# Merging page lists and gathering rows earlier in the last pages of a spectral mixture-of-experts kernel

## The chip, the cores and the metric

The kernel runs on one core of a Trainium2 chip. The metric is device time in microseconds, the median of several executions. Five engines work side by side, each through its own instructions in order: PE (TensorE, matrix multiplication), DVE (VectorE), ACT (ScalarE), POOL (GpSimd, which here issues the indirect transfers) and SP (SyncE, which issues most other transfers). PEld in the profile is the weight load of a matmul, which overlaps other matmuls.

## The reference

```python
def reference(**kwargs):
    # x: 8 x 3072 x 256
    X = np.fft.fft(x, axis=1); X = np.fft.fft(X, axis=2); x = X.real.reshape(24576, 256)
    # mixture of experts, top 1 of 8
    xn = x / (norm(x) + 1e-6); en = expert_emb / (norm(expert_emb) + 1e-6)
    logits = xn @ en.T / tau
    idx = argmax(logits); gate = softmax(logits)[idx]
    for e in range(8):
        out[idx == e] = gate * (relu(x[idx == e] @ w1[e]) @ w2[e])   # 256 -> 1024 -> 256
    # dense layer
    h = out @ w_in                                                   # 256 -> 2048
    return maximum(0.01 * h, h) @ w_out                              # 2048 -> 256
```

## The kernel before, in words

**Batches and routing.** For each of eight batches the transform is computed as matrix products, the result `xo` is stored to a table `xd` of 24576 rows in device memory, and each row is routed: its expert, its slot among that expert's rows and its gate are found, and three tables receive by scatter, at the row's slot, the row's number and gate. Each of the three holds a third of the entries; everywhere else stands a very large number.

**Pages.** A page is 256 slots of one expert. `load_page` (SP) reads the page's stretch of the three tables into a tile `t3`, `t` in the profile. `fetch_page` then does two things: DVE takes the minimum of the three (lines 872 and 873) and casts the row numbers to integers (line 878, tile `tab`), and POOL gathers the rows with an indirect transfer from `xd` into one of two buffers `xr`, 128 rows at a time (line 895). `transpose` turns the rows by PE (line 924) and splits them by ACT and DVE into a high and a low part (lines 926, 927, tile `xt`), since each product is made of three passes. 89 pages (`NFULL`) are full pages. What is left of the eight experts is computed in 21 half pages of 128 slots (numbers 89 to 109), with one gather each; their results pass through `yd` to seven last dense pages.

**Steps.** `steps` is a list of triples (kind, page, part). Kind 1 is the expert's layers of a full page, 4 steps; kind 3 those of a half page, 2 steps; kind 2 the dense layer, 8 steps. The loop goes over steps. At step `i` it first runs the hooks registered for `i`, then the first product of the step (kind 1: line 939, kind 2: line 1012, kind 3: line 971) with its work on ACT and DVE, then the second product (lines 957, 1043, 984) of the step three earlier (`LAG`). So PE does two groups of products in each step, and what ACT and DVE make of the first is needed three steps later. In kind 3 PE transposes the intermediate result as well (line 1028). From page 79 on, one full page and two half pages take turns: in the list of steps ten full pages (79 to 88) are at steps 944, 960, 976 and so on every 16, with a half page 7 and 12 steps behind each.

**Hooks.** For the page that is n-th in this order and begins at step `i`, `load_page` is registered at step `k`, 13 steps ahead of `i` (`AHEAD`) but not before the page before last has begun, or 7 ahead (`NEAR`) for the first ten. `fetch_page` follows by the line that the change touches. `transpose` stands at `i - 2`. The page's weights come as four pieces of 512 KB through two buffers `raw` (lines 906, 908, on SP, in the order of the hooks with the list loads) and are split by ACT and DVE (lines 917, 918) into `w1` and `w2`: for the full pages in turn with half pages the first two pieces at `i - 2` and `i - 1`.

An engine takes its instructions in the order in which the loop records them, so a hook's step sets the place on every engine that it uses.

Of the kernel before, what the change touches and what calls it, by code (L numbers as in the profile page):

```python
# [37 lines left out]
GAP = 1  # L38
# [20 lines left out]
class K:  # L59
# [770 lines left out]
    def main(self):  # L830
# [17 lines left out]
        for j in range(2, NFULL):  # L848
# [6 lines left out]
            if first <= j < NFULL - PRE + 1 and tail:  # L855
                left_pages = NFULL - PRE + 1 - j
                n = -(-len(tail) // left_pages)
# [199 lines left out]
        def at(i, fn, *args):  # L1057
            hooks.setdefault(max(0, i), []).append((fn, args))
# [3 lines left out]
        for n, (i, u) in enumerate(firsts):  # L1062
            ip_ = firsts[n - 1][0] if n else -8
            if n >= 2:
                k = max(firsts[n - 2][0] + 1, i - (NEAR if n < 10 else AHEAD))
                at(k, load_page, u)
                at(min(k + (GAP if n < 10 else 5), i - 3), fetch_page, u)
            if n:

                na = 4 if firsts[n - 1][1] < NFULL else 2  # L1070
                s0, s1 = ip_ + na, min(ip_ + na + 1, i)
                s2, s3 = ip_ + na // 2 + LAG + 1, min(ip_ + na + LAG, i + LAG)
                at(max(ip_ + 1, ls[0]), wload, u, 0)
                at(max(ip_ + 2, ls[1]), wload, u, 1)
                at(s0, wsplit, u, 0)
                at(s0, wload, u, 2)
                at(s1, wsplit, u, 1)
                at(s1, wload, u, 3)
                at(s2, wsplit, u, 2)
                at(s3, wsplit, u, 3)  # L1080
                ls = (s2, s3)
                at(max(i - 2, ip_ + na), transpose, u)
        last = firsts[-1][0]
        for t in range(NTF):
            i = [k for k, s in enumerate(steps) if s == (2, NU + t, 0)][0]
# [14 lines left out]
        with tc.tile_pool(name="ip", bufs=1) as self.ip:  # L1100
# [5 lines left out]
            for lab in g0:  # L1106
                n = count[lab] = count.get(lab, 0) + 1
                k, every = RAMP.get(lab, (0, 1))
# [61 lines left out]
        for i in range(len(steps) + LAG):  # L1170
# [8 lines left out]
            if i < len(steps):  # L1179
                m, u, s = steps[i]  # L1180
# [6 lines left out]
            while done < len(steps) and i - done >= (LAG if done > 4 * PRE else 2):  # L1187
                m, u, s = steps[done]
# [144 lines left out]
```

## Time and profile before

| | us |
|---|---|
| median of three runs | 3794.94 |
| lowest, highest | 3792.76, 3804.19 |
| profiled execution | 3783.82 |
| its span | 3782.1 |
| PE busy in the span | 3590.3 (95%) |
| DVE busy | 2338.3 (62%) |
| ACT busy | 1936.0 (51%) |
| POOL busy | 677.7 (18%) |

The mean granted clock of TensorE over the span is 0.971 of full speed. Busy time is summed over the whole span; what a stage waits for has to be read in that stage. In the rows, a bracket or the part behind the last bar tells how long an engine was idle before an instruction and what ended that. "SPq" is the issue of a transfer by SP.

### The profile page before, as it was taken

The numbers are of one execution on the slowest core, as the hardware profiler recorded it, in microseconds if no ns is written. First come the engines' busy times: TensorE is split into PE (matmuls) and PEld (weight loads), VectorE is DVE, ScalarE is ACT, GpSimd is POOL, SyncE is SP. The second block draws the span as 40 slices with busy tenths as digits, with TensorE's granted clock in tenths as the row PEclk, the third lists the DMA queues.
The fourth block names the chain that finished last, engine by engine and source line by source line (L and its number), as shares of the span: only waits on it lengthen the run. The fifth ranks groups of instructions, "written<-read, shape, count | busy, mean of one in ns | idle before, by whom it ended". The sixth has DMA issues, their size and how long they took to land. (4 is left out here: it accounts for less than half of the span.)

```text
span 3782.1 us, 74898 instructions
## 1 busy us (share of the span) xinstructions
PE 3590.3 (95%) x29441; PEld 3554.3 (94%) x29441; DVE 2338.3 (62%) x4595; ACT 1936.0 (51%) x3491; POOL 677.7 (18%) x620
## 2 busy tenths in 40 slices
PE   4488999999999999999999999999999999999998
PEld 3388999999999999999999999999999988988998
DVE  7575656567565666567565666657675556655544
ACT  3345446545555446455554456554645555555543
POOL 3113110411122101311023110311113111110000
PEclk8699999999999999999999999999999999999999
DMA  4332413232223223233233322232322244444300
GB/s 137 122 105 70 140 61 115 74 116 75 95 88 105 96 72 104 72 111 93 75 101 77 122 85 91 76 121 79 110 64 84 88 129 135 136 139 127 103 25 16
DMA packets 266165, 362.58 MB, mean 96 GB/s; under 512 B 75984, under 2 KB 216659, under 8 KB 265620
## 3 DMA queue, kind: packets, MB, share of 16 engines
q1 hardware_dynamic: 238896, 303.66, 25.6%
q0 software_dynamic: 25184, 52.35, 4.5%
q8 instruction: 230, 3.77, 0.4%
q10 hardware_dynamic: 1732, 1.79, 0.1%
q14 instruction: 123, 1.01, 0.1%
HBM read 304.64 MB, written 63.41 MB: 97 GB/s over the span
## 5 line engine op out<-in xcount | busy, mean ns | idle before, releaser
L1043 PE MATMUL o<-wo,hh 128*128 128x256 f32 x9216 | 1240.7, 284 | 10.1 <-DVE hh L1032 10.1
L1012 PE MATMUL h<-yt,wi 128*128 128x256 f32 x9216 | 1232.9, 283 | 13.5 <-ACT yt L961 13.4
L1043 PEld LDWEIGHTS o<-wo,hh 128*128 128x128 f32 x9216 | 1157.3, 190 | 13.8 <-DVE hh L1032 10.6
L1012 PEld LDWEIGHTS h<-yt,wi 128*128 128x128 f32 x9216 | 1152.5, 191 | 14.0 <-ACT yt L961 13.6
L1014 ACT ACTIVATE g<-h 128x512 f32<-128x512 f32 x768 | 457.8, 596 | 833.8 <-PE h L1012 827.8
L1015 DVE TENSOR_TENSOR g<-g,h 128x512 f32<-128x512 f32 x768 | 526.3, 685 | 509.7 <-ACT g L1014 508.7
L918 DVE TENSOR_TENSOR w<-raw,w 128x1024 fp32r<-128x1024 f32 x440 | 536.9, 1224 | 156.1 <-ACT w L917 153.3
L1050 POOL DMA_INDIRECT out<-ob,tab x192 | 216.9, 1130 | 2238.6 <-ACT ob L1049 1876.9
L942 DVE SCALAR_TENSOR_TENSOR hh<-h,hh 128x512 fp32r<-128x512 f32 x356 | 246.2, 692 | 559.7 <-ACT hh L941 558.3
L939 PE MATMUL h<-xt,w 128*128 128x256 f32 x4272 | 573.9, 284 | 16.4 <-ACT xt L926 14.0
L957 PE MATMUL y<-hh,w 128*128 128x256 f32 x4272 | 579.2, 285 | 8.5 <-ACT w L917 7.6
L939 PEld LDWEIGHTS h<-xt,w 128*128 128x128 f32 x4272 | 539.4, 192 | 18.0 <-ACT xt L926 14.9
L957 PEld LDWEIGHTS y<-hh,w 128*128 128x128 f32 x4272 | 541.5, 192 | 10.1 <-ACT w L917 8.0
L1032 DVE TENSOR_TENSOR hh<-g,hh 128x512 fp32r<-128x512 f32 x768 | 525.4, 684 | 1.1 <-ACT hh L1031 1.0
L917 ACT ACTIVATE w<-raw 128x1024 fp32r<-128x1024 f32 x440 | 461.8, 1054 | 85.5 <-DMA raw<-w 83.8
L1031 ACT ACTIVATE hh<-g 128x512 fp32r<-128x512 f32 x768 | 479.6, 625 | 25.4 <-DVE g L1015 25.3
L941 ACT ACTIVATE hh<-h 128x512 fp32r<-128x512 f32 x356 | 212.8, 598 | 529.0 <-PE h L939 528.9
L895 POOL DMA_INDIRECT xr<-xd,tab x199 | 235.9, 1185 | 685.1 <-issue 357.3
L597 POOL DMA_INDIRECT table<-tb,sli x192 | 217.8, 1135 | 170.3 <-DVE tb L591 56.6
L924 PE MATMUL a<-ident,xr 128*128 128x128 f32 x426 | 73.8, 290 | 81.9 <-DMA xr<-xd,tab 81.5
L924 PEld LDWEIGHTS a<-ident,xr 128*128 128x128 f32 x426 | 52.1, 146 | 87.1 <-DMA xr<-xd,tab 44.3
L1049 ACT ACTIVATE ob<-o,tf 128x256 f32<-128x256 f32 x192 | 80.6, 471 | 76.5 <-PE o L1043 76.4
(291 smaller groups left out, 1790.8 us busy)
## 6 DMA issues: line engine op xcount, KB each, us to landing
raw<-w SPq DMA_DIRECT2D x440, 512.0 KB
x<-xl SPq DMA_DIRECT2D x32, 768.0 KB
xd<-xo SPq DMA_DIRECT2D x96, 256.0 KB
table<-bigd SPq DMA_DIRECT2D x21, 384.0 KB
t<-table SPq DMA_DIRECT2D x267, 4.0 KB
xr<-xd,tab POOLq DMA_INDIRECT x199, 4.5
table<-tb,sli POOLq DMA_INDIRECT x192, 3.6
rawz<-w_out SPq DMA_DIRECT2D x6, 512.0 KB
```

The lines of the kernel that those rows point to most:

```text
L895: nc.gpsimd.indirect_dma_start(out=self.xr[seq[u] % NX][:, h], out_offset=None, in_=self.xd[0:rows, :], in_offset=bass.IndirectOffsetOnAxi ...
L917: nc.scalar.activation(hi, r, AF.Copy)
L918: V.tensor_tensor(lo, r, hi.bitcast(F32), op=ALU.subtract)
L939: nc.tensor.matmul(p[:, f], self.w1[:, wa, dc, fc * 128:(fc + 1) * 128], xt[:, xa, dc], start=(k == 0), stop=(k == 5))
L942: V.scalar_tensor_tensor(h[:, 1], p, 0.0, h[:, 0].bitcast(F32), op0=ALU.max, op1=ALU.subtract)
L957: nc.tensor.matmul(y[:, x], self.w2[:, wa, fc, xs_], h[:, ha, f], **st)
L1012: nc.tensor.matmul(p[:, f], self.wi[:, wa, dc, fc * 128:(fc + 1) * 128], yt[:, xa, dc], start=(k == 0), stop=(k == 5))
L1014: nc.scalar.activation(g, p, AF.Copy, scale=0.01)
L1015: V.tensor_tensor(g, g, p, op=ALU.max)
L1031: nc.scalar.activation(h[:, 0], g, AF.Copy)
L1032: V.tensor_tensor(h[:, 1], g, h[:, 0].bitcast(F32), op=ALU.subtract)
L1043: nc.tensor.matmul(o[:, th], h[:, xa, f, th * 128:(th + 1) * 128], self.wo[:, wa, fc], start=(fc == 0 and th == 0 and k == 0), stop=(fc == ...
```

## The change

The first ten pages in order keep their distance. From there on the row gather was registered five steps behind the list's load, at most three ahead of the page's first step; now it is eight steps ahead of the page's first step, or one step behind the load where that is later. 70 pages come out at the same step as before (13 ahead for the load, 8 for the gather). 31 pages move: ten full pages from 3 to 7 steps ahead (load at 8 ahead), ten half pages from 5 to 8 (load at 10) and eleven half pages from 6 to 8 (load at 11).

```diff
             if n >= 2:
                 k = max(firsts[n - 2][0] + 1, i - (NEAR if n < 10 else AHEAD))
                 at(k, load_page, u)
-                at(min(k + (GAP if n < 10 else 5), i - 3), fetch_page, u)
+                at(min(k + GAP if n < 10 else max(k + GAP, i - 8), i - 3), fetch_page, u)
```

`GAP` is 1. The instructions of PE, ACT and POOL stand in the same order as before, and so do SP's transfers; on DVE the three instructions of a merge move.

The first place is DVE around the merge of the second full page in turn (page 80, `t_39030`, eight columns because of two halves). Before, behind the weight splits of the half page (`w_130` is `w2`, `w_129` is `w1`):

```order
 L918 TENSOR_TENSOR w_130<-raw,w_130 128x1024 x2
 L1032 TENSOR_TENSOR hh<-g,hh 128x512
 L872 TENSOR_TENSOR tf<-t_39030 128x8
 L873 TENSOR_TENSOR tf<-tf,t_39030 128x8
 L878 CAST tab<-tf 128x4
 L1032 TENSOR_TENSOR hh<-a,hh 128x512
 L918 TENSOR_TENSOR w_129<-raw,w_129 128x1024
 L927 TENSOR_TENSOR xt<-a,xt 128x512
```

Now, at the same page, with the half page's own split and transposes (`128x2x128`) still to come:

```order
 L1032 TENSOR_TENSOR hh<-a,hh 128x512
 L918 TENSOR_TENSOR w_129<-raw,w_129 128x1024
 L872 TENSOR_TENSOR tf<-t_39030 128x8
 L873 TENSOR_TENSOR tf<-tf,t_39030 128x8
 L878 CAST tab<-tf 128x4
 L1015 TENSOR_TENSOR g<-g,h 128x512
 L1032 TENSOR_TENSOR hh<-a,hh 128x512
 L918 TENSOR_TENSOR w_129<-raw,w_129 128x1024
 L927 TENSOR_TENSOR xt<-a,xt 128x2x128
```

The merge moved from just ahead of the full page's own first weight split to behind the first weight split of the half page before it, four steps up.

The second place is DVE around the merge of the half page that follows a full page (page 91, `t_38570`). Before, among the splits of the full page's `w2`:

```order
 L918 TENSOR_TENSOR w_130<-raw,w_130 128x1024 x2
 L942 SCALAR_TENSOR_TENSOR hh<-h,hh 128x512
 L872 TENSOR_TENSOR tf<-t_38570 128x4
 L873 TENSOR_TENSOR tf<-tf,t_38570 128x4
 L878 CAST tab<-tf 128x2
```

Now, behind the second split of the full page's `w1`:

```order
 L918 TENSOR_TENSOR w_129<-raw,w_129 128x1024
 L872 TENSOR_TENSOR tf<-t_38570 128x4
 L873 TENSOR_TENSOR tf<-tf,t_38570 128x4
 L878 CAST tab<-tf 128x2
 L1015 TENSOR_TENSOR g<-g,h 128x512
```

This merge moved up by three steps, to a place ahead of the full page's first step.

## Rows read from the trace of the kernel before

**Rows 1.** Windows: length, busy time of five engines, granted clock, DMA share, GB/s.

```profile
2447.00:2950.00 503.00, 502.26 (x4237) 500.78 (x4236) 321.12 (x638) 261.44 (x468) 100.81 (x90) 1.00 0.30 91
3000.00:3560.00 560.00, 521.53 (x3942) 505.59 (x3942) 338.65 (x497) 311.40 (x490) 66.97 (x62) 0.94 0.44 133
3092.72:3096.09 3.37, 0.00 (x0) 0.00 (x0) 1.27 (x2) 1.06 (x1) 1.60 (x2) 0.90 0.77 230
3096.09:3102.91 6.82, 6.61 (x32) 6.33 (x33) 2.29 (x4) 2.74 (x4) 0.00 (x0) 0.55 0.25 81
```

**Rows 2.** Groups by line, 3000 to 3560: busy, mean ns, idle before.

```profile
L924 PE MATMUL a<-ident,xr 128*128 128x128 f32 x80 | 20.9, 358 | 38.5 <-DMA xr<-xd,tab 38.0
```

**Rows 3.** Timeline at one full page: start, length, engine, line, instruction, idle before.

```profile
3089.32 0.35 SPq L906 DMA_DIRECT2D raw<-w  x1
...
3091.06 1.66 PE L1043 MATMUL o<-wo,hh 128*128 128x256 f32 x12
...
3092.30 1.01 POOL L895 DMA_INDIRECT xr<-xd,tab  x1 [19.15 <-DVE tab L878]
3092.49 0.33 SPq L906 DMA_DIRECT2D raw<-w  x1
3093.46 1.06 ACT L917 ACTIVATE w<-raw 128x1024 fp32r<-128x1024 f32 x1 [1.42 <-DMA raw<-w]
3093.62 1.00 POOL L895 DMA_INDIRECT xr<-xd,tab  x1 [0.30 <-issue]
3094.55 1.23 DVE L918 TENSOR_TENSOR w<-raw,w 128x1024 fp32r<-128x1024 f32 x1 [1.79 <-ACT w L917]
...
3096.30 1.37 PE L924 MATMUL a<-ident,xr 128*128 128x128 f32 x4 [3.58 <-DMA xr<-xd,tab]
```

**Rows 4.** The gathers of line 895, 3000 to 3560.

```profile
DMA to landing us min/median/max: 2.8/3.7/4.5
```

**Rows 5.** Windows of the ten stretches: the first, the last, their sum.

```profile
3034.91:3048.24 13.33, 8.19 (x48) 7.80 (x45) 4.65 (x9) 4.77 (x7) 2.02 (x2) 0.74 0.43 130
...
3528.52:3540.16 11.64, 8.03 (x48) 7.53 (x46) 4.38 (x8) 4.77 (x7) 2.02 (x2) 0.71 0.48 153
sum 119.75, PE 81.28 PEld 76.71 DVE 45.16 ACT 47.64 POOL 20.20; mean PE 8.13 PEld 7.67 DVE 4.52 ACT 4.76 POOL 2.02
```

**Rows 6.** Timeline at the half page before that full page.

```profile
3071.70 1.40 SPq L887 DMA_DIRECT2D t<-table  x3
...
3077.74 1.23 DVE L918 TENSOR_TENSOR w<-raw,w 128x1024 fp32r<-128x1024 f32 x1 [0.25 <-ACT w L917]
...
3078.74 0.60 PE L1028 MATMUL a<-ident,g 128*128 128x128 f32 x4
...
3079.10 1.68 PE L1043 MATMUL o<-wo,hh 128*128 128x256 f32 x12
...
3080.61 0.38 PE L924 MATMUL a<-ident,xr 128*128 128x128 f32 x2
...
3080.75 1.64 PE L1012 MATMUL h<-yt,wi 128*128 128x256 f32 x12
...
3082.23 1.60 PE L984 MATMUL y<-w,hh 128*128 128x256 f32 x12
...
3083.66 1.57 PE L1012 MATMUL h<-yt,wi 128*128 128x256 f32 x12
```

**Rows 7.** Timeline of PE at a last dense page.

```profile
3598.03 0.60 PE L924 MATMUL a<-ident,xr 128*128 128x128 f32 x4
3598.39 1.65 PE L1012 MATMUL h<-yt,wi 128*128 128x256 f32 x12
```

**Rows 8.** Line 872 over the span, and its timeline at one early page.

```profile
  DMA t<-table: 35.5, 5
...
490.25 1.40 SPq L887 DMA_DIRECT2D t<-table  x3
...
494.04 0.17 DVE L872 TENSOR_TENSOR tf<-t 128x8 f32<-128x8 f32 x1 [0.19 <-DMA t<-table]
```

## The prediction

> **What bounds the kernel now.** I read the stages first. Between 2447 and 2950 us TensorE (PE) is busy 502.26 of 503.00 us at a granted clock of 1.00, and between 3000 and 3560 us, where half pages are interleaved with the last ten full pages, it is busy 521.53 of 560.00 us at 0.94 [rows 1]. So the kernel is bound by PE nearly everywhere, and this one stage has something to give back: 38.47 us of idle time, and a lower clock besides. Second, the groups by line of the same stage: the transposes of gathered rows (line 924) have 38.5 us of PE's idle time in front of them, 38.0 of it ended by the gather `xr<-xd,tab` [rows 2]. No other line is left with any. Third, one of these waits in order of time [rows 3]: PE's group before the transposes starts at 3091.06 and is over 1.66 us later, GpSimd (POOL) starts the two gathers of a full page only at 3092.30 and 3093.62, and PE starts its transposes at 3096.30. A gather takes 3.7 us (median) from issue to landing [rows 4]. The list is merged by VectorE (DVE) one step before the transposes, and a step on PE is two groups of about 1.43 us (3082.23 to 3083.66) [rows 6]. Waiting is not all: while PE idles (3092.72 to 3096.09) the granted clock is 0.90, and in the 6.82 us behind that 0.55, mostly 1.2 instead of 2.4 GHz; in the stage before it is 1.00 [rows 1]. Fourth, ten such stretches, one for each full page of the stage, together: 119.75 us, of which PE is busy for 81.28 [rows 5]. The difference, 38.47 us, is all the idle time of the stage, so there is no second cause in it.
>
> **What moves.** The diff concerns only pages from the eightieth on; worked out with the table of steps, 31 change: ten full pages go from three steps ahead to seven, ten half pages from five to eight, eleven half pages from six to eight. Per page that is three short DVE instructions (line 872, 873, 878) and one or two gathers. Their number stays; the order of PE, ScalarE (ACT), POOL and of SyncE's (SP) DMAs stays too. Only DVE's order changes. POOL's gather has the same neighbours, so it simply becomes ready sooner.
>
> **The gain at one full page.** I count from the start of the group of line 1043 before the transposes to the start of the next step's first group. In the ten places this took 119.75 us together, 13.33 in the first and 11.64 in the last [rows 5]. Undisturbed, the same instructions take: line 1043 behind transposes 1.51 (3079.10 to 3080.61), four row transposes 0.36 (3598.03 to 3598.39), line 1012 behind them 1.48 (3080.75 to 3082.23), the four transposes of line 1028 0.36 (3078.74 to 3079.10), line 1043 again 1.51: 5.22 us [rows 6, 7]. The loss is 119.75 - 10 x 5.22 = 67.6 us: 38.0 of waiting and about 29.6 of work at the lower clock.
>
> The Trainium skill, TensorE: Matmul & The Clock Gate, section on HAM oscillation, prices the same thing as throttled time times one half, on top of the wait. By that rule the stage loses 560 x 0.06 = 34 us of clock and 38.5 of waiting, 72 in all. I keep 67.6, since part of the lowered clock falls into the waiting itself (0.90 in the idle stretch) and costs nothing there; the trace agrees with the rule otherwise.
>
> **Is the gather early enough afterwards?** In the place shown, the merge now stands behind the weight split of line 918 that began at 3077.74 and ended at 3078.97 [rows 6], so gathers start near 3080.0 and 3081.3 and have landed, by 3.7 and the longest 4.5 [rows 4], by about 3086. PE wants them at 3092.57 (3091.06 + 1.51): some 6 us to spare. Half pages had no wait before and get more room: nothing to win there.
>
> **Does the merge now wait for its list?** It stands one step behind the list's loads. SP issued these at 3071.70, far ahead of the step they belong to [rows 6]; in another place a merge that just caught its list began 3.79 us after the first of three loads (490.25 to 494.04) [rows 8]. So the list is there by about 3075.5 and the slot comes at 3078.97: 3.5 us to spare, and zero is my value for the wait. Behind the merge DVE has `g` and `hh` of two steps, which PE needs three steps later; the merge itself delays these by 0.55 us, hidden there. The bound above is the start of the kernel, where five merges waited 35.5 us together [rows 8]. Below nothing there is no gain, as DVE is not what PE waits for in this stage.
>
> **What is late next.** The same full page needs its first weights. Of its two pieces the second was issued at 3092.49; the first took 4.14 us from issue to use (3089.32 to 3093.46) [rows 3]. So it would be split by ACT from 3096.63, by DVE 1.09 later for 1.23, and be ready at 3098.95. Undisturbed, PE starts the page two groups after the stretch: 3091.06 + 5.22 + 2 x 1.43 = 3099.1. That is just in time, and the last weights are only used at the sixth matmul of the group. The first of the ten places is 1.4 us longer than their mean (13.33 against 11.98), so its transfers came later; I take half a microsecond there and nothing elsewhere, with 22 us in all as the far end (below). The gathers now run beside other weight loads, the half page's last two; ACT has them split three steps before PE's use, so I cost that at nothing.
>
> **Sum.** 3783.82 us (the profiled execution, span 3782.1) - 67.6 + 0.5 = 3716.7. The median of the runs shown is 11.1 us above that execution, and I leave this offset: 3794.94 - 67.1 = 3727.8, say 3728 us.
>
> **Rivals.**
> - The wait turns into one for weights: each full page's second piece is late. For: the chain above has only 0.2 us of slack, and SP issues three list loads between the two pieces. Against: with the gathers gone the piece has the DMA queues more to itself. Price: if all ten are late by the first place's 1.4 us, PE idles 1.4 - 0.2 = 1.2 us, with the clock's share (67.6 / 38.0 = 1.8 times) 2.2 us, ten times: 22 us back, 3750 us.
> - It does not do what it says, and the gather is still held, by its buffer or by POOL's queue. Against: the two row buffers are freed by the transposes of the page before last, eleven or more steps ahead, and POOL's order has no scatter between. Time: 3795 us.
> - Slower: the merge waits for its list, as at the kernel's start, and DVE, which works in order, holds back `g` and `hh` for PE. For: those early pages also have the merge one step behind the load and waited 7.1 us on average (35.5 / 5) [rows 8]. Against: there SP itself came late; here it is 7.3 us ahead of the slot. It decides once a list lands more than 7.3 us after its first issue. Price at all 31 moved pages, without any slack: 31 x 7.1 = 220 us, so 3728 + 220 = 3948 us.
>
> **How the numbers follow.** Forecast 0.80, weights 0.12, nothing 0.04, slower 0.04. A measurement of this kernel tells 0.3% (11.4 us) from no change. The range goes from the forecast less that uncertainty, 3715, to the weights' case with a little more, 3757, and holds the first two. Both are faster by over 0.3%: 0.92; same 0.04; slower 0.04.
>
> **What would show it.** Right: PE idle in the last stage under 5 us, granted clock 1.00 there, a full page every 48.1 us instead of 54.8 ((3528.52 - 3034.91) / 9 [rows 5], less 6.76), no DVE wait on line 872 there. Wrong: idle time before line 939 or 957 ended by `w`, or before 872 ended by `t<-table`, or the ten waits on line 924 still there. If the waits are gone and the time has not moved by 50 us or more, my price of the clock is wrong.

## The result and the profile after

The changed kernel takes 3732.47 us (median of 4 runs, 3725.53 to 3735.78), against 3798.27 us for the kernel before (4 runs, 3792.76 to 3804.19): a ratio of 0.9824, interval 0.9802 to 0.9846. Forecast were 3728 us and a range of 3715 to 3757. The profiled execution took 3731.02 us with a span of 3729.3 us.

All of it is in one stage. I measure that stage in every kernel between two events that all of them have: the first row transpose of page 78, the last full page that the change leaves alone, and that of page 109, the last half page. Before, this took 571.26 us. The pages that move in it are 30, not 31: in the two profiles 30 merges stand at another place in the order of VectorE (DVE), those of the ten full pages, of nine half pages (from five steps ahead to eight) and of eleven (from six to eight). The first half page, 89, stays where it was. The windows of the kernel before, with the columns of [rows 1]:

```profile
2988.88:3560.14 571.26, 532.79 (x4038) 516.85 (x4037) 344.46 (x510) 315.88 (x497) 67.97 (x63) 0.94 0.43 130
```

The windows of the changed kernel, the stage first, then the first and the second of the ten stretches of [rows 5], with the sum of all ten:

```profile
3003.89:3507.34 503.45, 503.45 (x4038) 492.06 (x4037) 341.96 (x509) 313.71 (x497) 76.86 (x63) 1.00 0.51 148
...
3049.92:3055.12 5.20, 5.20 (x47) 5.20 (x46) 2.30 (x3) 3.50 (x6) 0.00 (x0) 1.00 0.58 181
3097.94:3103.15 5.21, 5.21 (x47) 5.21 (x46) 2.48 (x4) 3.61 (x7) 0.00 (x0) 1.00 0.66 204
...
sum 52.06, PE 52.06 PEld 52.06 DVE 24.75 ACT 36.99 POOL 0.00; mean PE 5.21 PEld 5.21 DVE 2.48 ACT 3.70 POOL 0.00
```

Read the first three numbers: TensorE (PE) is busy for every one of 503.45 us, with the same 4038 matmuls, at a granted clock of 1.00 where it was 0.94. The stage is 67.81 us shorter, and the ten stretches, 119.75 us before [rows 5], are 52.06: 67.69 us of the 67.81. The group of the transposes, which had 38.5 us of idle time in front of it [rows 2], has none; their mean is 272 ns instead of 358 (groups by line, 3000 to 3560 us):

```profile
L924 PE MATMUL a<-ident,xr 128*128 128x128 f32 x90 | 15.2, 272 | 0.0
```

One full page of the changed kernel in order of time, the counterpart of [rows 3] and of the half page in [rows 6]. In this timeline and in those below, rows of other instructions are left out:

```profile
3084.62 1.23 DVE L918 TENSOR_TENSOR w<-raw,w 128x1024 fp32r<-128x1024 f32 x1 [0.25 <-ACT w L917]
3085.76 0.16 DVE L872 TENSOR_TENSOR tf<-t 128x8 f32<-128x8 f32 x1
...
3086.16 0.17 DVE L878 CAST tab<-tf 128x4 int32<-128x4 f32 x1
...
3087.11 1.02 POOL L895 DMA_INDIRECT xr<-xd,tab  x1 [12.36 <-PE a L1028]
...
3087.89 1.23 DVE L918 TENSOR_TENSOR w<-raw,w 128x1024 fp32r<-128x1024 f32 x1
3088.43 1.56 POOL L895 DMA_INDIRECT xr<-xd,tab  x1 [0.30 <-issue]
...
3097.94 1.66 PE L1043 MATMUL o<-wo,hh 128*128 128x256 f32 x12
...
3099.38 0.33 SPq L906 DMA_DIRECT2D raw<-w  x1
3099.44 0.60 PE L924 MATMUL a<-ident,xr 128*128 128x128 f32 x4
...
3103.04 1.06 ACT L917 ACTIVATE w<-raw 128x1024 fp32r<-128x1024 f32 x1 [0.26 <-DMA raw<-w]
...
3104.30 1.22 DVE L918 TENSOR_TENSOR w<-raw,w 128x1024 fp32r<-128x1024 f32 x1
...
3105.98 1.60 PE L939 MATMUL h<-xt,w 128*128 128x256 f32 x12
```

The merge stands behind the half page's first weight split, the second gather is issued 11.0 us before PE's transposes (2.7 us before), and PE goes from line 1043 into the transposes with no idle time. The second weight piece is split by 3105.52, and PE wants the page at 3105.98: 0.46 us. The releaser in the first gather's row is inferred: line 1028 ran at about the same moment, but what the gather reads is the `tab` that the cast finished at 3086.33.

Behind page 109 both kernels take 221.96 us to the end. The two spans nevertheless differ by only 52.8 us, because page 78 came at 3003.89 us in this profile and at 2988.88 in the one of before: 67.81 - 15.01 = 52.80. Up to that row transpose PE, DVE, ACT and POOL have the same instructions in both kernels, in the same order, so these 15 us are not the change's (last section). The medians of the runs differ by 65.8 us.

### The profile page after: what moved, and what is told of

It is laid out like the page before. It is cut to its first block, busy times and chain, and to the rows that moved or that the text cites. A ratio compares the mean times of both kernels' runs of the same rounds, so it can differ in the third digit from the quotient of the medians.

```text
span 3729.3 us, 74898 instructions
## 1 busy us (share of the span) xinstructions
PE 3568.1 (96%) x29441; PEld 3531.2 (95%) x29441; DVE 2338.1 (63%) x4595; ACT 1933.1 (52%) x3491; POOL 677.0 (18%) x620
## 3 DMA queue, kind: packets, MB, share of 16 engines
q1 hardware_dynamic: 238896, 303.66, 26.5%
q14 instruction: 123, 1.01, 0.1%
## 5 line engine op out<-in xcount | busy, mean ns | idle before, releaser
L895 POOL DMA_INDIRECT xr<-xd,tab x199 | 245.3, 1233 | 547.2 <-issue 303.6
L597 POOL DMA_INDIRECT table<-tb,sli x192 | 208.9, 1088 | 162.8 <-issue 53.8
L924 PE MATMUL a<-ident,xr 128*128 128x128 f32 x426 | 66.3, 274 | 36.7 <-DMA xr<-xd,tab 36.7
L926 ACT ACTIVATE xt<-a 128x512 fp32r<-128x512 f32 (+1 forms) x110 | 61.0, 555 | 71.1 <-PE a L924 68.9
```

The lines of the kernel that those rows point to most:

```text
L895: nc.gpsimd.indirect_dma_start(out=self.xr[seq[u] % NX][:, h], out_offset=None, in_=self.xd[0:rows, :], in_offset=bass.IndirectOffsetOnAxi ...
```

## The experiments

All have the stage's length as their finest measure. For the kernels below it is in each case the first number behind the window.

**e1: full pages alone.** Only the ten full pages go up, the half pages keep the old distance.

```
- at(min(k + (GAP if n < 10 else 5), i - 3), fetch_page, u)
+ at(min(k + GAP if n < 10 else max(k + GAP, i - 8) if u < NFULL else k + 5, i - 3), fetch_page, u)
```

> Only the ten full pages are merged and gathered seven steps ahead; the 21 half pages stay where they were. The measure is the stage from the row transposes of page 78 to those of page 109: 571.3 us in the kernel before, 503.5 in the changed one. Theory A (all of the gain is the gather's wait at the ten full pages and the clock behind it): 503 to 505 us, ratio to the kernel before about 0.982. Theory B (the half pages' earlier gathers or the new order on VectorE give a part): at least 5 us longer, 508 or more, ratio 0.984 to 0.99.

Measured: 3730.86 us, ratio 0.9821 (0.9805 to 0.9838). The stage of e1:

```profile
2995.29:3498.74 503.45, 503.45 (x4038) 492.06 (x4037) 340.31 (x509) 313.60 (x497) 73.42 (x63) 1.00 0.50 148
```

To the hundredth that of the changed kernel. The ten full pages are the whole gain.

**e2: half pages alone.** The same line with `u >= NFULL`; it moves 20 half pages, since page 89 stays.

> Only the 21 half pages are moved, the ten full pages keep three steps. Theory A: 570 to 572 us for the stage (571.3 before), ten waits of 3.2 to 5.1 us still in front of the transposes, ratio 1.000 within the noise. Theory B: shorter by 5 us or more, ratio 0.998 or less.

Measured: 3795.8 us, ratio 0.9998 (0.9986 to 1.0009). The stage of e2 and, from the groups by line, its transposes:

```profile
3001.11:3570.50 569.39, 530.97 (x4039) 514.86 (x4037) 346.27 (x510) 315.79 (x497) 66.47 (x63) 0.94 0.44 131
```

```profile
L924 PE MATMUL a<-ident,xr 128*128 128x128 f32 x86 | 22.1, 354 | 38.4 <-DMA xr<-xd,tab 38.2
```

All ten waits are still there. Moving the half pages is worth nothing that the times show, as the prediction said; the stage of the one profile is 1.9 us shorter, with the same waits.

**e3: full pages one step earlier than before.** If the wait is a matter of lead, part of the gain should come with one step.

```
- at(min(k + (GAP if n < 10 else 5), i - 3), fetch_page, u)
+ at(min(k + (GAP if n < 10 else 5), i - 4 if u < NFULL else i - 3), fetch_page, u)
```

> Full pages are gathered one step earlier than before (four ahead instead of three), half pages stay. One step is 2.86 us, so of a wait of 3.85 us on average about 1 us is left at each of the ten pages. Theory A, with the clock following the length of the idle time: about 10 us of idle time and no lower clock, stage 512 to 516 us, granted clock 1.00, ratio about 0.985. Rival (the clock falls behind any such wait, however short): 10 us of idle time and nearly all of the 29.6 us of slower work, stage about 540 us, clock 0.95, ratio 0.992.

Measured: 3792.78 us, ratio 0.9987 (0.9975 to 1.0), with 37.1 us of waits. The stage of e3:

```profile
3008.97:3577.76 568.79, 531.67 (x4039) 516.04 (x4038) 344.17 (x510) 315.50 (x497) 67.82 (x63) 0.95 0.44 131
```

This expectation was wrong: nearly all of the waiting is still there. The timeline of e3 at the second full page shows why:

```profile
3106.93 2.36 DVE L918 TENSOR_TENSOR w<-raw,w 128x1024 fp32r<-128x1024 f32 x2 [0.82 <-ACT w L917]
3109.20 0.16 DVE L872 TENSOR_TENSOR tf<-t 128x8 f32<-128x8 f32 x1
3110.56 1.01 POOL L895 DMA_INDIRECT xr<-xd,tab  x1 [18.56 <-DVE hh L1032]
3111.88 1.00 POOL L895 DMA_INDIRECT xr<-xd,tab  x1 [0.30 <-DVE hh L1032]
...
3114.47 0.33 PE L924 MATMUL a<-ident,xr 128*128 128x128 f32 x1 [2.90 <-DMA xr<-xd,tab]
3115.90 0.55 PE L924 MATMUL a<-ident,xr 128*128 128x128 f32 x3 [1.11 <-DMA xr<-xd,tab]
```

One step up, the merge is still queued behind VectorE's (DVE's) two splits of the half page's second weights (2.36 us), which themselves wait for ScalarE. Its place moved past one instruction only, the work of line 1032, 0.6 us. A step of the program is not a time on the engine: the reading is that what counts is which instruction stands ahead in DVE's queue, and e9 and e10 put it to the test.

**e9: full pages two steps earlier.** The revised theory says that the next step, which passes the two splits, brings everything at once.

```
- at(min(k + (GAP if n < 10 else 5), i - 3), fetch_page, u)
+ at(min(k + (GAP if n < 10 else 5), i - 5 if u < NFULL else i - 3), fetch_page, u)
```

> Full pages gathered two steps earlier than before (five ahead), half pages as before. After the run with one step, which moved the merge on VectorE by only 0.6 us since it stayed behind the two weight splits of line 918 (2.36 us), the theory is now: what counts is the merge's place in VectorE's queue, not the step. Five ahead it stands before those splits, in front of the work of line 1015, about 6 us earlier on VectorE than in the kernel before; the gathers then land 1.5 to 2 us before the transposes. Expected: no wait, clock 1.00, stage from page 78 to page 109 503 to 505 us, ratio 0.982. Rival (the number of steps counts, 2.86 us each, and the first of the two gave nothing): at most one more step is won, stage 530 us or more.

Measured: 3732.34 us, ratio 0.9828 (0.9805 to 0.9851), no waits left. The timeline of e9 at the same page, and its stage:

```profile
3091.43 0.16 DVE L872 TENSOR_TENSOR tf<-t 128x8 f32<-128x8 f32 x1
3092.78 1.01 POOL L895 DMA_INDIRECT xr<-xd,tab  x1 [12.46 <-PE h L1012]
3094.10 1.19 POOL L895 DMA_INDIRECT xr<-xd,tab  x1 [0.31 <-DVE g L1015]
3095.23 2.36 DVE L918 TENSOR_TENSOR w<-raw,w 128x1024 fp32r<-128x1024 f32 x2 [0.82 <-ACT w L917]
...
3099.72 0.60 PE L924 MATMUL a<-ident,xr 128*128 128x128 f32 x4
```

```profile
3004.15:3507.62 503.47, 503.47 (x4038) 492.08 (x4037) 340.08 (x509) 312.92 (x497) 71.79 (x63) 1.00 0.51 148
```

Ten pages merged two steps earlier do all that the change does, which moves them by four; the other two buy room only.

**e10: e3's step, but ahead of the splits within it.** This holds the step fixed and changes only the order of DVE in it.

```
- at(min(k + (GAP if n < 10 else 5), i - 3), fetch_page, u)
+ if n >= 79 and u < NFULL:
+     hooks.setdefault(i - 4, []).insert(0, (fetch_page, (u,)))
+ else:
+     at(min(k + (GAP if n < 10 else 5), i - 3), fetch_page, u)
```

> Full pages gathered four ahead, as in the run with one step, but recorded before the two weight splits of the same step instead of behind them; nothing else differs from it. Theory (VectorE's queue): the merge comes about 3.1 us earlier than in the kernel before and falls into idle time of VectorE; the second gather lands about 1 to 1.4 us after the transposes could start. Stage 511 to 518 us, idle time about 10 to 14 us; if the clock follows the length of the idle time it stays at 1.00. Rivals: the place within a step does not count, stage 569 us as with one step; or the clock falls behind short waits too, stage 530 us or more.

Measured: 3762.01 us, ratio 0.99 (0.9878 to 0.9922). The stage of e10, and one page in order of time:

```profile
3007.41:3543.44 536.03, 515.21 (x4038) 499.85 (x4037) 343.60 (x510) 314.88 (x497) 78.69 (x63) 0.98 0.47 139
```

```profile
3099.56 0.16 DVE L872 TENSOR_TENSOR tf<-t 128x8 f32<-128x8 f32 x1
3100.46 2.36 DVE L918 TENSOR_TENSOR w<-raw,w 128x1024 fp32r<-128x1024 f32 x2 [0.34 <-ACT w L917]
3100.92 1.67 POOL L895 DMA_INDIRECT xr<-xd,tab  x1 [15.37 <-PE h L971]
3102.74 0.68 DVE L1032 TENSOR_TENSOR hh<-g,hh 128x512 fp32r<-128x512 f32 x1
3102.89 1.42 POOL L895 DMA_INDIRECT xr<-xd,tab  x1 [0.30 <-DVE w L918]
...
3106.55 0.33 PE L924 MATMUL a<-ident,xr 128*128 128x128 f32 x1 [1.44 <-DMA xr<-xd,tab]
3107.84 0.55 PE L924 MATMUL a<-ident,xr 128*128 128x128 f32 x3 [0.97 <-DMA xr<-xd,tab]
```

In the same step, ahead of the splits instead of behind them, the merge saves 32.8 us of the stage against e3 (568.79 - 536.03). So the order in DVE's queue is a cause, shown. The size was missed: 536 is above what I expected. Waits of 20.8 us are left, 2.1 a page. GpSimd (POOL) needs 1.67 and 1.42 us for two gathers that took 1.01 and 1.00 before [rows 3], the first while DVE runs the splits, the second while it runs line 1032: 1.1 of the 2.1 us, which I had not counted (last section). The rest of the stage's excess, 536.03 - 503.45 - 20.8 = 11.8 us, goes with a clock of 0.98. The rival that short waits lower the clock too came true in five of the ten places, where the granted clock of the 7 us from the first transpose on is 0.76; in the other five it is 1.00.

**e4: the waits stay, but PE works through them.** The kernel before, with 26 matmuls that nothing uses ahead of the row transposes of pages 79 to 88. If the price beyond the waiting is the clock, it should go, though the gather is as late as ever.

```
- def split_t(x, tag, bufs, n=2):
-     pt = self.ps("a", [128, 512], 2).rearrange("p (c t) -> p c t", c=2)[:, :, 0:128 * n]
+ def split_t(x, tag, bufs, n=2, fill=0):
+     pt = self.ps("a", [128, 512], 2)
+     for _ in range(fill):
+         nc.tensor.matmul(pt[:, 0:256], self.wi[:, 0, 0, 0:128], self.wo[:, 0, 0], start=True, stop=True)
+     pt = pt.rearrange("p (c t) -> p c t", c=2)[:, :, 0:128 * n]
...
- xts[u] = split_t(self.xr[seq[u] % NX], "xt", 1, 2 if u < NFULL else 1)
+ xts[u] = split_t(self.xr[seq[u] % NX], "xt", 1, 2 if u < NFULL else 1, 26 if NFULL > u >= 79 else 0)
```

> The kernel before, with 26 extra matmuls (128 columns of weights, 256 columns moving, result thrown away) ahead of the row transposes of the ten full pages in turn with half pages, that is 3.1 us of work on TensorE in place of most of the wait. The gather stays as late as it was. Theory A (29.6 of the 67.6 us are the lower clock that idle time brings): the wait's 38 us stay as filler and rest, the clock stays at 1.00, stage about 542 us (571.3 - 29.6), ratio about 0.992. Rival (what is slow behind the wait is slow for another cause, such as the transfers or the engines that have to catch up): stage 571 us, ratio 1.000.

Measured: 3773.55 us, ratio 0.9927 (0.9911 to 0.9944), a stage of 554.38 us at 0.99. The ten stretches of e4, the second, the last and their sum:

```profile
3099.38:3108.95 9.57, 8.76 (x74) 8.37 (x72) 4.03 (x8) 4.30 (x7) 2.02 (x2) 1.00 0.60 195
...
3522.20:3534.75 12.55, 10.32 (x73) 9.92 (x72) 4.27 (x8) 4.45 (x7) 2.02 (x2) 0.86 0.46 143
sum 102.86, PE 90.55 PEld 86.75 DVE 41.13 ACT 43.76 POOL 20.21; mean PE 9.05 PEld 8.68 DVE 4.11 ACT 4.38 POOL 2.02
```

The filler is 10 x 26 matmuls of 0.119 us (twelve take 1.43), 31.0 us, and 12.1 us of waiting for the gather are left. Of the excess over the undisturbed stage, 554.38 - 503.45 = 50.9, that leaves 7.8 us; in the kernel before it was 67.8 - 38.0 = 29.8. The work added is rather more than 31.0: at full clock a stretch has 8.76 us of busy time against 5.21 undisturbed, 3.55 us a place, by which 3.3 us are left. With PE busy the clock stays at 1.00 in eight of the ten places, at 0.86 in the last two, and 22 to 26.5 of the 29.8 us are gone. More work made the kernel quicker: the second term of the prediction's sum is for the most part the clock's. That filler and rest (43.1 us at least) come to more than the 38.0 us of wait they replace, and the two last places, are why the stage is longer than I expected.

**e5: the merge in the very step of the list's load.** `max(k, i - 8)` in place of `max(k + GAP, i - 8)`: the slower rival, provoked.

> The changed kernel, with the ten full pages merged and gathered in the very step of the list's load, one step earlier still. Theory (the list is there about 3.5 us before the slot of the changed kernel, since SyncE issues it ahead of its step): the slot comes one step, up to 2.9 us, earlier, so there is 0.6 us to spare or a wait of at most 1 us on VectorE, hidden from TensorE by the three steps between the products; stage 503 to 505 us, ratio to the kernel before 0.982. Rival (a merge this near to its load waits as the early pages do, and holds TensorE up): ten waits of line 872 of several us each, stage 540 us or more.

Measured: 3731.56 us, ratio 0.9816 (0.9792 to 0.984). The stage of e5:

```profile
3010.74:3514.19 503.45, 503.45 (x4038) 492.06 (x4037) 342.07 (x509) 313.46 (x497) 71.72 (x63) 1.00 0.50 148
```

PE is never idle in it. One merge in the stage waits for its list, by 0.40 us and on DVE alone, within the 1 us that I had allowed:

```profile
3089.01 0.17 DVE L872 TENSOR_TENSOR tf<-t 128x8 f32<-128x8 f32 x1 [0.40 <-DMA t<-table]
```

So one step nearer to the load the room is used up, but ten waits of several us, as the rival had it, do not come: it is refuted for these pages.

**e8: GAP = 2.** In the changed line GAP holds for the early pages as well, so here these merge two steps behind their list. It also moves the ten full pages, from seven steps ahead to six. It asks whether the list waits at the start [rows 8] are worth anything.

> The changed kernel with the first ten pages merged two steps behind their list's load instead of one. Theory (the waits of line 872 at the start, 35.5 us in five, are not what TensorE waits for there): the waits shrink, the time stays within 0.3% of the changed kernel, ratio to the kernel before 0.980 to 0.985. Rival (a merge that waits for its list costs TensorE time there): up to 12 us faster, 0.979, or slower if a gather now comes late for one of these pages.

Measured: 3741.45 us (3738.64 to 3745.27), ratio 0.9847 (0.9825 to 0.9869). The waits on the list fell as meant, to 12.8 us in 2; the stage is 503.45 us. The ratio lies within what I expected, but the kernel is 9.9 us slower than e5, and all four of its runs lie above all of e5's. Its profile shows where: between 295 and 560 us, at the early pages, the row transposes wait for the gather (waits of PE in that window: us in total, times, longest; e8, then e5).

```profile
PE a L924 <- DMA xr<-xd,tab: 9.6, 4, 6.2
PE a L924 <- DMA xr<-xd,tab: 1.1, 1, 1.1
```

So the second half of the rival is what happened: with its merge a step later the gather is late for some of these pages. What the shorter waits on the list are worth can't be read apart from that; in sum the kernel lost.

## Why the prediction was right

- **The loss at a full page** held. Predicted were 5.22 us for the undisturbed stretch and 67.6 us of loss in ten; measured 5.21 (52.06 / 10) and 67.7. Working out the undisturbed length from the same groups elsewhere in the trace [rows 6, 7], rather than from the idle time alone, is what brought in the second half of the gain: by idle time alone it would have been 38 us. e4 shows that most of this half is the clock's. The rule of the Trainium skill, TensorE: Matmul & The Clock Gate, section on HAM oscillation, would have given an estimate of 72 us; the stage lost 67.8. The reason that the prediction gives for the difference has the right sign: over the ten waits of the kernel before, 38.0 us, the granted clock averages 0.85, so some 5.7 us of the lowered clock fell where PE stood still.
- **The gather comes early enough**: right. Its second piece was issued 11.0 us ahead of the transposes; I had 3092.57 - 3081.3 = 11.3.
- **The merge does not wait for its list**: right. The list waits over the whole span are 16.8 us in 4, all at the kernel's start; e5, at one step less, has one of 0.40 us in the stage. The view of line 872 of the changed kernel, the counterpart of the first of [rows 8]:

```profile
  DMA t<-table: 16.8, 4
```

- **What is late next**: right in place, slightly too dear. I called the second weight piece just in time, with 0.2 us of slack, and took 0.5 us of waiting at the first place. In the ten places the split ended 0.03 to 0.66 us before PE's start, and there was no wait: the stage has no idle time. The room is wider than that, since what this split makes is first used at the sixth matmul of the group, 0.60 us after its start (five of 0.119): in e9 the split ended 0.47 us behind PE's start at the first place (3057.46 + 1.23 against 3058.21), and PE had no idle time there either. So the first rival (3750 us) was avoided by 0.6 to 1.3 us a page. That the next saving on PE in this stage would meet these weights is likely, but no run tests it.
- **The period of a full page**: 48.03 us ((3483.66 - 3051.42) / 9), predicted 48.1.
- **The total**: 3727.8 predicted, 3732.47 measured, 4.7 us more. The base, the median of before, moved from 3794.94 to 3798.27 with the fourth run, 3.3 us; and the medians differ by 65.8 us instead of 67.1, 1.3 us, although the stage gained 67.81, 0.7 more than predicted. Taking the gain off the median, and not off the profile, was needed: as a forecast of the next profile, 3716.7 was 14.3 us too low, namely 15.01 us of the time before page 78 less those 0.7.
- **The number of pages**: wrong. 30 move, not 31, so the slower rival's price would have been 30 x 7.1 = 213 us. Nothing else hangs on it.
- **A phrase that misled**: "one step before the transposes" was true of the program's text, and e3 shows what it hid. The gather was late because of DVE's queue, not because of the number of steps; the prediction did not need this, as the change passed the splits anyway, but my expectation of e3 did, and failed.

## What to carry to other kernels

Count the lead of a transfer in the queue of the engine that makes its addresses, not in steps of the loop: one step brought 2.5 us of the stage, the second all the rest. Price a short wait of TensorE by the whole stretch around it against the same groups undisturbed, since the work behind the wait may run at the lower clock; here 38 us of waiting cost 68. And before you believe a gain, look at what is late next: here the next weights were ready 0.03 to 0.66 us before PE began the page.

## What the runs showed of the hardware that was not expected

- **Gathers that begin during a split.** In the stage a gather on POOL took 1.00 us (median; 1.37 at most) in the kernel before and 1.32 (2.01 at most) in the changed one. Beside VectorE's (DVE's) splits of line 918, what counts is which began first. Two of e5's gathers:

```profile
3091.47 1.22 DVE L918 TENSOR_TENSOR w<-raw,w 128x1024 fp32r<-128x1024 f32 x1 [0.25 <-issue]
3091.70 1.87 POOL L895 DMA_INDIRECT xr<-xd,tab  x1 [0.30 <-issue]
...
3139.43 1.00 POOL L895 DMA_INDIRECT xr<-xd,tab  x1 [0.30 <-issue]
3139.49 1.23 DVE L918 TENSOR_TENSOR w<-raw,w 128x1024 fp32r<-128x1024 f32 x1 [0.25 <-ACT w L917]
```

The one that began before the split took 1.00 us; the one that began during it ended 0.88 us after the split (3093.57 against 3092.69). In the stages of nine profiles, all but e4's, 56 gathers began during a split, and all ended 0.87 to 0.93 us after it; 27 that began with VectorE idle, and during which a split began, took 0.99 to 1.05 us; four that began with the split took 1.05. The second gather of e10 ended 0.89 us after line 1032 (rows above). PE had no idle time from it in the changed kernel's stage; in e10 it had.
- **Short waits can lower the clock.** In e10 pairs of waits as short as 0.89 and 1.04 us, with 0.33 us of work between them, ended in a stretch at a lower clock in five of the ten places. The sums of the two waits, 1.9 to 2.6 us there and 1.1 to 2.5 us in the other five, do not tell the places apart.
- **The same instructions, 22 us apart.** Up to the first row transpose of page 78 PE, DVE, ACT and POOL have the same instructions in the same order in all kernels but e8, and yet that page came between 2988.88 us (before) and 3010.74 (e5) in nine profiles. Between the two main profiles PE was busy 2846.14 against 2853.23 us in that part, and idle for 142.7 against 150.7; in the changed kernel some of it stands as idle time that nothing in the profile ends. The view of waits of that kernel (line, what it waited for, us in total, times, longest):

```profile
PE o L1043 <- issue: 11.2, 18, 1.8
PE h L1012 <- issue: 9.2, 20, 1.0
```

What these are, the profile doesn't say. The profile of the kernel before has no such line; all the others have 14.7 to 20.8 us of them. So it is that profile, at 3783.82 us below all of the kernel's runs, that stands apart. For reading such a pair of profiles it means: compare the stage, not the span.
